# Spectral mixing and a bilinear GLU on one core: left-over rows stacked from group 3 on instead of 5, in five sets with their own scratch

## The chip, the core and the metric

The kernel runs as one launch on one core of a Trainium2 chip. The metric is device time in microseconds of that launch. The kernel before was timed three times: 671.66, 671.69 and 671.91 us, median 671.69 us. The profile is of another execution of the same program, which took 671.72 us; its span, from the first to the last instruction, is 669.9 us.

Engines are named as in the profile: PE is TensorE (matmuls), PEld its weight loads, DVE VectorE, ACT ScalarE, POOL GpSimd, SP SyncE. SP computes nothing; it issues transfers in program order, and a transfer that has to wait holds back all transfers written behind it.

## What is computed

Two blocks in sequence on x of shape (2048, 640) in float32. The first is layer normalisation, a real 2-D Fourier transform, a pointwise product with a complex filter, the inverse transform and the residual. The second is layer normalisation, a bilinear gated unit with 1728 hidden columns, and the residual.

```python
def _A_ref(x, w_r, w_i):
    X = jnp.fft.rfft2(x, axes=(-2, -1))
    X = X * (w_r + 1j * w_i)
    return jnp.fft.irfft2(X, s=(S, D), axes=(-2, -1))

def _B_ref(x, w_gate, w_up, w_down):
    h = jnp.einsum("bsd,df->bsf", x, w_gate) * jnp.einsum("bsd,df->bsf", x, w_up)
    return jnp.einsum("bsf,fd->bsd", h, w_down)

h  = x + _A_ref(_layernorm(x), A_w_r, A_w_i)
h2 = h + _B_ref(_layernorm(h), B_w_gate, B_w_up, B_w_down)
```

The change lies in the first block alone, in the transform along the 640 features.

## The kernel before

The sequence of 2048 rows is split as 16 times 128. A first stage transforms along 128 (the matmuls of line 270, to about 38 us of the span). Its result is cut into 16 **groups** of frequencies. The **feature stage** (about 38 to 100 us) then runs a loop over the groups g = 0 to 14, and each pass does for PE, in this order:

- `s2_mm(g)`, line 476: the transform along 16, from the tile `t` into the PSUM tile `u`. There is one `u` only, so this may write it no sooner than DVE has read the last one.
- `d_mm(g + 2)`, line 121 by the helper `mmx`: the transform along the 640 features. Folding has cut it into four "main" products of 128 rows (tile `s1`, tables `tab`), and a small rest of rows that don't fill 128. The rest is done in fp32r (a split into a high and a low part, three products).
- `is2_mm(g - 1)`, line 527: the inverse along 16, into `ir` (64 + 1 rows) and `im`.

DVE does `filt(g)` (lines 484 to 486: three products of `u` with the filter `wts`), the sum at line 493, and line 563. ACT copies `d_mm`'s result to `t` (line 465) and the inverse's result away (lines 545 and 556). So the loop is closed: `u` is written by PE, read by three DVE operations, and only then written again.

The rest of rows in `d_mm` exists in two forms:

- **Plain** (groups 0 to 4, `g < PLAIN`): six matmuls over 128 rows and 322 columns, read from `s1r`, which holds the high part in plane 0 and the low part in plane 1. The 128 rows are four quarters of 31 to 33 rows, and each quarter belongs to its own 160 to 194 columns of `re` or `im`; for the others the table holds zeros.
- **Stacked** (groups 5 to 15): the rows of one quarter are brought together three times over, as 33 high, 33 low and 33 high rows on 99 partitions. One matmul of 160 to 194 columns for each quarter then does the three products: four short matmuls instead of six long ones.

To stack rows on other partitions, they go through device memory. `spread(a, b)` writes the 33 rows of both planes for a range of groups to the scratch `sfar`, four transfers from SP, one for each quarter (line 445). `stack(g, n, tag)` reads n groups back, 66 partitions and 33 partitions in two transfers (line 455). The scratch is one tensor of shape [4 quarters, 2 planes, 33 rows, 11 groups, 128]; so one partition that is read gathers, for each quarter, a run of n x 512 bytes.

The order is written out by hand, and all these transfers are on SP's queue. Beside them SP issues for each pass two transfers of `bits` (the matrices of lines 476 and 527, line 417) and one or two of `wts` (the filter, lines 410 and 412). SP has eight semaphores for its transfers, used in turn: transfer k waits until transfer k - 8 has landed.

Before the loop, three pairs of ACT and DVE operations (lines 300 and 303) make the high and low parts of `s1r` for groups 0-1, 2-4 and 5-9, and a fourth pair, inside the loop, that of groups 10-15. `spread(5, 10)` is issued ahead of the loop, `stack` for groups 5-7 in pass 0, for groups 8-9 in pass 1, `spread(10, 16)` in pass 2, `stack` for 10-12 in pass 4 and for 13-15 in pass 7:

```python
PLAIN, MID = 5, 10
AGAIN = {0: (5, 3, "dC"), 1: (8, 2, "qt"), 4: (10, 3, 0), 7: (13, 3, 1)}
```

A tag names where the stacked rows stand in SBUF: `dC` and `qt` are free tiles, 0 and 1 are the two planes of `s1r` itself, whose groups 4 to 15 are overwritten once they have been spread.

Of the kernel before, what the change touches and what calls it, by code (L numbers as in the profile page):

```python
# [11 lines left out]
F32 = mybir.dt.float32  # L12
# [4 lines left out]
P = 128  # L17
S, D, NF, FF = 2048, 640, 321, 1728
NT = S // P
NG = 16  # L20
# [4 lines left out]
RROWS = ((31, 1), (0, 1), (62, 2), (63, 2))  # L25
RWHERE = ((1, 0), (0, 0), (1, 160), (0, 160))
RW = (160, 194, 162, 162)
PLAIN, MID = 5, 10
IPLAIN, IFAR = 5, 9
SUMS = 7  # L30
IPARTS = ((5, 4), (9, 3), (12, 4))
AGAIN = {0: (5, 3, "dC"), 1: (8, 2, "qt"), 4: (10, 3, 0), 7: (13, 3, 1)}
NR = 4
AHEAD = 5
FOLDS = {0: (1, 2), 1: (3,), 2: (4,), 7: (9,), 9: (11,)}
# [14 lines left out]
def f32(ap):  # L50
    return ap.bitcast(F32)
# [29 lines left out]
def tile_spectral_glu(ctx: ExitStack, tc: tile.TileContext, x, wre, wim, wgu, wlast, wdown, wdlast,  # L81
                      cc, ci, fmain, frem, imain, irem, mm, out):
    nc = tc.nc
# [4 lines left out]
    far = ctx.enter_context(tc.tile_pool(name="far", bufs=1, space=bass.MemoryType.DRAM))  # L88
# [60 lines left out]
    s1r = home("wA", [P, 2, NG, P], "s1r", F32R)  # L149
# [142 lines left out]
    def s1_rest(t):  # L292
        act(at(rest, t), PS1[t][1][:, 0:P].rearrange("p (g m) -> p g m", g=32), AF.Copy)
# [5 lines left out]
    def rest_high(a, b):  # L299
        act(s1r[:, 0, a:b], rest[:, a:b], AF.Copy)  # L300

    def rest_low(a, b):
        tt(s1r[:, 1, a:b], rest[:, a:b], f32(s1r[:, 0, a:b]), op=OP.subtract)
# [94 lines left out]
        s1_mm(t)  # L398
    s1_main(NT - 1, PS1[NT - 1][0], 2, 4)
    s1_rest(NT - 1)  # L400
    for a, b in ((0, 2), (2, PLAIN), (PLAIN, MID)):
        rest_high(a, b)
        rest_low(a, b)

# [2 lines left out]
    def load_w(g):  # L407
        w, j = wts[:, g % 3], g // 2 if g < NG - 2 else g - 7
        i = wts[:, 5 if j == 8 else 3 + j % 2]
        nc.sync.dma_start(w, wre[g])  # L410
        if g % 2 == 0 or g >= NG - 2:
            nc.sync.dma_start(i, wim[j])
        W2[g] = w, i

    def load_mm(g, way):
        if g < NG:
            nc.sync.dma_start(mms[g % 4][:, way], mm[g][:, way])
# [22 lines left out]
    ST = {}  # L440
    sfar = far.tile([4, 2, 33, NG - PLAIN, P], F32, name="sfar")

    def spread(a, b):
        for q, (r, s) in enumerate(RROWS):
            nc.sync.dma_start(sfar[q, :, :, a - PLAIN:b - PLAIN].rearrange("l r g n -> r l g n"),
                              f32(s1r[r:r + 32 * s + 1:s, :, a:b]))

    def stack(g, n, tag):
        if tag in (0, 1):
            o = s1r[:, tag, NG - 12:NG].rearrange("p (q n) m -> p q n m", q=4)  # L450
        else:
            o = home(tag, [P, 4, n, P], "st", F32R)
        src = sfar[:, :, :, g - PLAIN:g - PLAIN + n].rearrange("q l r g n -> q (l r) (g n)")
        for a, b, r in ((0, 66, 0), (66, 99, 0)):
            nc.sync.dma_start(f32(o[a:b].rearrange("p q g n -> p q (g n)")),
                              src[:, r:r + b - a].rearrange("q r n -> r q n"))
        for i in range(n):
            ST[g + i] = o[:, :, i]

    def d_out(g, parts=(0, 1)):  # L460
        for i in parts:
# [5 lines left out]
    def s2_mm(g):  # L467
        if g >= NG - 2:
            ps = PU[g] = bank("re"), bank("im")
        elif g == 0:  # L470
            ps = PU[g] = bank("im2", 1), bank("ir2", 1)
        else:
            PU[g] = pools["y"].tile([P, 2, 512], F32, tag="u", name="u", bufs=1)
            ps = PU[g][:, 0], PU[g][:, 1]
        for h in range(2):
            nc.tensor.matmul(ps[h][:, 0:NQ], mms[g % 4][:, 0, h], T[g][:, h], start=True, stop=True)  # L476
# [106 lines left out]
    for g in range(NG - 1):  # L583
        s2_mm(g)
        load_mm(g + 4, 0)
        if g + 2 < NG:
            d_mm(g + 2)
        if g + 3 == NG:
            xt = home("big", [P, 2, 5, 2, 512], "xt", F32R)
            flat = xt[:, 1].rearrange("p k l n -> p (k l n)")  # L590
            irt, sirt = cut(flat, 0, 5, NQ), cut(flat, 5 * NQ, 4, 162)
            scrap, near = cut(flat, 2258, D), cut(flat, 2258 + D, 4, 4, P)
        if g == NG - 2:
            nc.gpsimd.dma_start(flat[:, 0:2258], irem)
        if g == NG - 2:
            s2_mm(g + 1)
            filt_half(g, 0, True, (lambda: is2_out(g - 2),))
        if g >= 1:
            is2_mm(g - 1)
            load_mm(g + 3, 1)  # L600
        if g < NG - 2:
            add = filt(g)
        else:
            direct, _ = filt_half(g, 1)
            direct()
            late = [filt_half(g + 1, 0), filt_half(g + 1, 1, True)]
            high, end, low, main, edges = is2_parts(g - 1)
            late[0][0]()
            high(copy)
            end(copy)  # L610
            low()
            late[0][1]()
            late[1][1]()
            main(slice(0, 4))
            edges(nc.gpsimd)
        if g + 3 < NG:
            load_w(g + 3)
        if g >= 4 and g in AGAIN:
            stack(*AGAIN[g])
        if g == 0:  # L620
            rest_high(MID, NG)
        elif g == 1:
            rest_low(MID, NG)
            qr = home("qr", [P, 2, NT, P], "qr", F32R)
        if g + 2 < NG:
            d_out(g + 2, (0,))
            if 1 <= g < NG - 3:
                high, end, low, main, edges = is2_parts(g - 1)
                high(copy)
                end(copy)  # L630
            d_out(g + 2, (1,))
            add()
            if 1 <= g < NG - 3:
                low()
                main(slice(0, 4))
                edges(nc.gpsimd)
        if g < 2:
            stack(*AGAIN[g])
        elif g == 2:
            spread(MID, NG)  # L640
        if g == 9:
            nc.sync.dma_start(cit, ci)
            nc.sync.dma_start(imt, imain)
# [252 lines left out]
    for ts in (range(3), range(3, 6), range(6, 8)):  # L896
        n, t0 = len(ts), ts[-1] + 1
# [664 lines left out]
```

## Time and profile before

| what | value |
|---|---|
| median of three runs | 671.69 us |
| the profiled execution, whole | 671.72 us |
| its span | 669.9 us |
| granted TensorE clock | 0.999 of full speed |
| feature stage | about 38 to 100 us of the span |
| moved by DMA over the whole span | 66.12 MB in 48953 packets |

The profile has a page (busy time by engine, a chain of the work that ended last, groups of instructions) and views that are asked for: a timeline of one engine in order of time, busy time by window, and a table of waits. A row of a timeline reads: start in us, length in us, engine, line, operation, what it writes and from what, shape, count, and in brackets the idle time ahead of it with what ended it. SPq rows are the issuing of transfers, not the moving of bytes. Names such as `sfar<-s1r` are the program's tiles; `frt` and `tab` are tables.

### The profile page before, as it was taken

What the parts mean: (1) busy time and instruction counts of PE and PEld (TensorE: products, weight loads), DVE (VectorE), ACT (ScalarE), POOL (GpSimd) and SP (SyncE); (2) the same over time, 40 slices, a digit from 0 to 9 for tenths busy, and PEclk for the clock granted to TensorE, in tenths of its full rate; (3) what the DMA queues carried; (4) which work ended last, traced back from release to release, by engine and by line L of the source; (5) the groups of instructions that cost most, each with busy time, mean ns of one, the idle gap of its engine ahead of it and who ended that gap; (6) DMA issues with size and microseconds to landing.
All of it is one profiled execution on the core that took longest, in us unless ns stands there. A gap on an engine that the chain in (4) does not pass through costs nothing.

```text
span 669.9 us, 10244 instructions
## 1 busy us (share of the span) xinstructions
PE 661.1 (99%) x3695; PEld 588.4 (88%) x3695; DVE 469.1 (70%) x953; ACT 321.6 (48%) x621; POOL 394.1 (59%) x377
## 2 busy tenths in 40 slices
PE   7999999999999999999999999999999999999997
PEld 7999999887888888888888899888888888888887
DVE  6969997788767767594857567754757475757644
ACT  6977773585525244453626146534434251624220
POOL 3101124750397977968696445198786869697610
PEclk9999999999999999999999999999999999999999
DMA  8638874502212120142332467212011121212004
GB/s 316 230 111 279 245 250 144 172 2 79 79 40 80 39 79 21 33 105 60 98 79 83 95 132 261 79 40 73 14 37 75 41 78 40 79 40 80 1 0 158
DMA packets 48953, 66.12 MB, mean 99 GB/s; under 512 B 24082, under 2 KB 30670, under 8 KB 48774
## 3 DMA queue, kind: packets, MB, share of 16 engines
q1 hardware_dynamic: 48246, 62.91, 30.4%
q0 software_dynamic: 288, 2.16, 0.8%
q8 instruction: 29, 0.48, 0.3%
q10 hardware_dynamic: 368, 0.39, 0.2%
q14 instruction: 22, 0.18, 0.1%
HBM read 54.61 MB, written 10.84 MB: 98 GB/s over the span
## 4 chain that ended last, share of the span: by engine, by line
PE 95%; ACT 2%; DVE 2%; DMA 1%; issue 0%; DVEq 0%
PE e L121 50%; PE d L121 26%; PE eo L121 4%; PE y L121 2%; PE re L121 2%; PE u L476 2%; PE im L121 2%; PE im L527 2%; PE im L270 2%; PE ir L527 1%; DMA x<-in_x_dram 1%; ACT s L296 1%; ACT fold L212 0%; ACT fold L211 0%; PE y L803 0%
## 5 line engine op out<-in xcount | busy, mean ns | idle before, releaser
L121 PE MATMUL e<-xt,wst 128*128 128x512 f32 x864 | 211.1, 390 | 0.0
L121 PEld LDWEIGHTS e<-xt,wst 128*128 128x128 f32 x864 | 160.6, 188 | 31.7
L1082 DVE TENSOR_TENSOR x<-d,x 128x320 f32<-128x320 f32 x280 | 120.3, 482 | 41.2 <-PE d L121 37.0
L121 PE MATMUL d<-wd,ht 128*128 128x320 f32 x832 | 142.1, 309 | 0.0
L121 PEld LDWEIGHTS d<-wd,ht 128*128 128x128 f32 x832 | 129.6, 188 | 5.2
L996 POOL TENSOR_TENSOR wst<-raw,wst 128x1024 fp32r<-128x1024 f32 x23 | 55.5, 2412 | 69.4 <-ACT wst L995 69.4
L121 PE MATMUL e<-t,wst 128*128 128x512 f32 x360 | 94.0, 391 | 0.0
L121 PEld LDWEIGHTS e<-t,wst 128*128 128x128 f32 x360 | 66.7, 188 | 13.0
L121 PE MATMUL d<-wt,ht 128*128 128x320 f32 x360 | 68.9, 309 | 0.0
L1012 POOL TENSOR_TENSOR wst<-raw,wst 128x896 fp32r<-128x896 f32 (+1 forms) x46 | 65.3, 1445 | 0.2 <-ACT wst L1007 0.2
L121 PEld LDWEIGHTS d<-wt,ht 128*128 128x128 f32 x360 | 57.3, 188 | 0.8
L1098 ACT ACTIVATE ht<-e 128x512 fp32r<-128x512 f32 x44 | 26.4, 600 | 49.3 <-DVE e L1160 23.7
L1007 ACT ACTIVATE wst<-raw 128x896 fp32r<-128x896 f32 (+1 forms) x48 | 30.1, 676 | 31.2 <-POOL raw L1001 30.4
L1156 DVE TENSOR_TENSOR e<-e,h 128x512 f32<-128x512 f32 x24 | 16.8, 699 | 39.4 <-ACT wst L1007 23.2
L1057 DVE TENSOR_TENSOR x<-d,x 128x320 f32<-128x320 f32 x62 | 27.5, 485 | 22.5 <-PE d L121 22.4
L688 ACT ACTIVATE wd<-draw 128x320 fp32r<-128x320 f32 (+1 forms) x30 | 15.7, 561 | 55.2 <-POOL draw L698 52.4
L121 PE MATMUL e<-xt,wdir 128*128 128x512 f32 x180 | 41.9, 392 | 0.0
L1136 ACT ACTIVATE h<-e 128x512 f32<-128x512 f32 x24 | 14.3, 596 | 56.8 <-PE e L121 56.8
L121 PEld LDWEIGHTS e<-xt,wdir 128*128 128x128 f32 x180 | 33.4, 188 | 7.5 <-ACT xt L813 0.5
L1101 DVE TENSOR_TENSOR ht<-e,ht 128x512 fp32r<-128x512 f32 x54 | 36.9, 685 | 1.6 <-ACT ht L1098 1.3
L1153 ACT ACTIVATE h<-e 128x512 f32<-128x512 f32 x24 | 14.3, 597 | 46.6 <-PE e L121 46.6
L667 POOL TENSOR_TENSOR wd<-draw,wd 128x640 fp32r<-128x640 f32 x8 | 12.5, 1582 | 40.8 <-ACT wd L666 40.8
(241 smaller groups left out, 1190.6 us busy)
## 6 DMA issues: line engine op xcount, KB each, us to landing
raw<-in_wgu_dram SPq DMA_DIRECT2D x24, 640.0 KB
draw<-in_wdown_dram SPq DMA_DIRECT2D x24, 320.0 KB
wts<-in_wre_dram SPq DMA_DIRECT2D x16, 322.0 KB
x<-in_x_dram SPq DMA_DIRECT2D x15, 320.5 KB
out_dram<-x SPq DMA_DIRECT2D x15, 320.0 KB
bits<-in_mm_dram SPq DMA_DIRECT2D x32, 128.0 KB
wts<-in_wim_dram SPq DMA_DIRECT2D x9, 322.0 KB
zfar<-zr SPq DMA_DIRECT2D x32, 80.0 KB
```

The costliest lines, as they stand in the source:

```text
L121: nc.tensor.matmul(o, l, r, start=start, stop=stop, skip_group_check=True)
L527: nc.tensor.matmul(out, y[:, h, a:b], inv(g, h), start=n == 0, stop=n == len(ys) - 1)
L688: act(o[:, 0, a:a + n], src, AF.Copy)
L996: ptt(wa[:, 1], stage[:, 0:1024], f32(wa[:, 0]), op=OP.subtract)
L1007: act(ws[:, 0, o:o + b - a], stage[:, a:b], AF.Copy)
L1012: ptt(ws[:, 1, o:o + b - a], stage[:, a:b], f32(ws[:, 0, o:o + b - a]), op=OP.subtract)
L1057: tt(xv, ps[b][:, 0:320], xv, op=OP.add)
L1082: tt(xv, o, xv, op=OP.add)
L1098: act(hop[:, a, 0], src, AF.Copy)
L1101: engine.tensor_tensor(hop[:, a, 1], src, f32(hop[:, a, 0]), op=OP.subtract)
L1136: act(h0, oa, AF.Copy)
L1156: tt(ob, ob, h1, op=OP.add)
```

## The change

Stacking starts at group 3 instead of group 5. The eleven, now thirteen, stacked groups are cut into five sets (3-5, 6-7, 8-10, 11-13, 14-15), and each set has a scratch tensor of its own, in the order [plane, row, quarter, group, 128]. A partition that is read then finds its four quarters in one run of n x 2048 bytes, where before there were four runs of n x 512. The transfers of `spread` write runs of n x 512 bytes, n being 3 or 2, where before they wrote 5 x 512 and 6 x 512.

```diff
-PLAIN, MID = 5, 10
+PLAIN, NEXT, MID = 3, 6, 10
-AGAIN = {0: (5, 3, "dC"), 1: (8, 2, "qt"), 4: (10, 3, 0), 7: (13, 3, 1)}
+SETS = ((3, 3, "dC"), (6, 2, "qt"), (8, 3, 0), (11, 3, 1), (14, 2, "dC"))
+SPREAD, AGAIN = {1: (2,), 2: (3, 4)}, {1: 1, 3: 2, 6: 3, 8: 4}
...
-    for a, b in ((0, 2), (2, PLAIN), (PLAIN, MID)):
+    for a, b in ((0, 2), (PLAIN, NEXT), (2, PLAIN), (NEXT, MID)):
         rest_high(a, b)
         rest_low(a, b)
...
-    sfar = far.tile([4, 2, 33, NG - PLAIN, P], F32, name="sfar")
+    sfar = [far.tile([2, 33, 4, n, P], F32, name="sfar") for _, n, _ in SETS]
 
-    def spread(a, b):
+    def spread(i):
+        g, n, _ = SETS[i]
         for q, (r, s) in enumerate(RROWS):
-            nc.sync.dma_start(sfar[q, :, :, a - PLAIN:b - PLAIN].rearrange("l r g n -> r l g n"),
-                              f32(s1r[r:r + 32 * s + 1:s, :, a:b]))
+            nc.sync.dma_start(sfar[i][:, :, q].rearrange("l r g n -> r l g n"),
+                              f32(s1r[r:r + 32 * s + 1:s, :, g:g + n]))
...
-        src = sfar[:, :, :, g - PLAIN:g - PLAIN + n].rearrange("q l r g n -> q (l r) (g n)")
+        src = sfar[i].rearrange("l r q g n -> (l r) (q g n)")
         for a, b, r in ((0, 66, 0), (66, 99, 0)):
-            nc.sync.dma_start(f32(o[a:b].rearrange("p q g n -> p q (g n)")),
-                              src[:, r:r + b - a].rearrange("q r n -> r q n"))
+            nc.sync.dma_start(f32(o[a:b].rearrange("p q g n -> p (q g n)")), src[r:r + b - a])
...
-    spread(PLAIN, MID)
+    spread(0)
+    stack(0)
+    spread(1)
...
-        if g >= 4 and g in AGAIN:
-            stack(*AGAIN[g])
+        if g >= 3 and g in AGAIN:
+            stack(AGAIN[g])
...
-        if g < 2:
-            stack(*AGAIN[g])
-        elif g == 2:
-            spread(MID, NG)
+        if g == 1:
+            stack(AGAIN[g])
+        for i in SPREAD.get(g, ()):
+            spread(i)
```

Three places of the instruction order matter. The first is PE in pass 1, `d_mm(3)`, from its last main product to the first product of `is2_mm(0)`. Before:

```order
L121 MATMUL re_634<-tab_87,s1_89 128x161
L121 MATMUL re_634<-frt_88,s1r_90 128x322
L121 MATMUL im_635<-frt_88,s1r_90 128x322
L121 MATMUL re_634<-frt_88,s1r_90 128x322
L121 MATMUL im_635<-frt_88,s1r_90 128x322
L121 MATMUL re_634<-frt_88,s1r_90 128x322
L121 MATMUL im_635<-frt_88,s1r_90 128x322
L527 MATMUL ir2_647<-bits_94,y_611 65x32x4 x2
```

And the same place now (`st` is the tile of the stacked rows):

```order
L122 MATMUL re_644<-tab_87,s1_89 128x161
L122 MATMUL im_645<-frt_88,st_566 128x160
L122 MATMUL re_644<-frt_88,st_566 128x194
L122 MATMUL im_645<-frt_88,st_566 128x162
L122 MATMUL re_644<-frt_88,st_566 128x162
L529 MATMUL ir2_655<-bits_94,y_624 65x32x4 x2
```

Six long matmuls have become four short ones, which read `st` where the six read `s1r`. The same holds for `d_mm(4)`, one pass later.

The second place is SP's queue from the end of the load of the first matrices to the second read of stacked rows. Before:

```order
L445 DMA sfar_542<-s1r_90 33x2x640 x4
L417 DMA bits_94<-in_mm_dram 128x256
L410 DMA wts_93<-in_wre_dram 128x644
L455 DMA st_627<-sfar_542 66x4x384
L455 DMA st_627<-sfar_542 33x4x384
L417 DMA bits_94<-in_mm_dram 128x256 x2
L410 DMA wts_93<-in_wre_dram 128x644
L412 DMA wts_93<-in_wim_dram 128x644
L455 DMA st_676<-sfar_542 66x4x256
L455 DMA st_676<-sfar_542 33x4x256
```

Now:

```order
L447 DMA sfar_544<-s1r_90 33x2x384 x4
L458 DMA st_566<-sfar_544 66x1536
L458 DMA st_566<-sfar_544 33x1536
L447 DMA sfar_545<-s1r_90 33x2x256 x4
L418 DMA bits_94<-in_mm_dram 128x256
L411 DMA wts_93<-in_wre_dram 128x644
L418 DMA bits_94<-in_mm_dram 128x256 x2
L411 DMA wts_93<-in_wre_dram 128x644
L413 DMA wts_93<-in_wim_dram 128x644
L458 DMA st_684<-sfar_545 66x1024
L458 DMA st_684<-sfar_545 33x1024
```

The first read of stacked rows has moved ahead of a transfer of `bits` and one of `wts`, to right behind the writes that it waits for; four writes of a second set have come in between.

The third place is SP's queue behind that, up to the read of the set of groups 8 to 10. Now:

```order
L447 DMA sfar_546<-s1r_90 33x2x384 x4
L418 DMA bits_94<-in_mm_dram 128x256 x2
L411 DMA wts_93<-in_wre_dram 128x644
L447 DMA sfar_547<-s1r_90 33x2x384 x4
L447 DMA sfar_548<-s1r_90 33x2x256 x4
L418 DMA bits_94<-in_mm_dram 128x256 x2
L411 DMA wts_93<-in_wre_dram 128x644
L413 DMA wts_93<-in_wim_dram 128x644
L458 DMA s1r_90<-sfar_546 66x1536
L458 DMA s1r_90<-sfar_546 33x1536
```

Before, one set of four writes stood here (of 768 columns), and no read: groups 8 and 9 had been read already, and the next read was that of groups 10 to 12, a pass later. On ACT and DVE one operation of lines 300 and 303 has become two (640 columns are now 128 and 512), and groups 3-5 come second in their order.

More of the change, by code (lines that the diff above doesn't have):

```diff
@@ L440, in tile_spectral_glu, with stack @@
     ST = {}
-    sfar = far.tile([4, 2, 33, NG - PLAIN, P], F32, name="sfar")
-    def spread(a, b):
+    sfar = [far.tile([2, 33, 4, n, P], F32, name="sfar") for _, n, _ in SETS]
+    def spread(i):
+        g, n, _ = SETS[i]
         for q, (r, s) in enumerate(RROWS):
-            nc.sync.dma_start(sfar[q, :, :, a - PLAIN:b - PLAIN].rearrange("l r g n -> r l g n"),
-                              f32(s1r[r:r + 32 * s + 1:s, :, a:b]))
-    def stack(g, n, tag):
+            nc.sync.dma_start(sfar[i][:, :, q].rearrange("l r g n -> r l g n"),
+                              f32(s1r[r:r + 32 * s + 1:s, :, g:g + n]))
+    def stack(i):
+        g, n, tag = SETS[i]
         if tag in (0, 1):
@@ L452, in stack @@
             o = home(tag, [P, 4, n, P], "st", F32R)
-        src = sfar[:, :, :, g - PLAIN:g - PLAIN + n].rearrange("q l r g n -> q (l r) (g n)")
+        src = sfar[i].rearrange("l r q g n -> (l r) (q g n)")
         for a, b, r in ((0, 66, 0), (66, 99, 0)):
-            nc.sync.dma_start(f32(o[a:b].rearrange("p q g n -> p q (g n)")),
-                              src[:, r:r + b - a].rearrange("q r n -> r q n"))
-        for i in range(n):
-            ST[g + i] = o[:, :, i]
+            nc.sync.dma_start(f32(o[a:b].rearrange("p q g n -> p (q g n)")), src[r:r + b - a])
+        for j in range(n):
+            ST[g + j] = o[:, :, j]
     def d_out(g, parts=(0, 1)):
```

## The prediction

> **What bounds the kernel now.** I read the page first: busy time by engine, then the chain of the work that ended last. Then I went to the feature stage alone, by windows and by the timeline of one engine.
>
> ```profile
> PE 661.1 (99%) x3695; PEld 588.4 (88%) x3695; DVE 469.1 (70%) x953; ACT 321.6 (48%) x621; POOL 394.1 (59%) x377
> PE 95%; ACT 2%; DVE 2%; DMA 1%; issue 0%; DVEq 0%
> 48.74:53.20 4.46, 4.46 (x33) 1.00 0.85 250
> 57.17:61.16 3.99, 3.99 (x31) 1.00 0.83 284
> ```
>
> PE is busy 99% of the span and is 95% of the chain, so a microsecond taken from PE is a microsecond of the kernel, unless something else is late next. The last two rows are PE alone (length, busy, granted clock, DMA share, GB/s): a pass with a plain `d_mm` takes 4.46 us, one with a stacked `d_mm` 3.99 us, at full clock. Two plain passes become stacked. But DMA engines are 85% busy there, and DVE has work of its own. Here is PE from `d_mm(3)` (plain) to the fourth `u`:
>
> ```profile
> 47.74 0.42 PE L121 MATMUL re<-frt,s1r 128*128 128x322 f32 x1
> 48.74 0.60 PE L527 MATMUL ir<-bits,y 128*65 128x128 f32 x4
> 50.07 1.25 PE L476 MATMUL u<-t,bits 128*128 128x322 f32 x4
> 54.52 1.25 PE L476 MATMUL u<-t,bits 128*128 128x322 f32 x4
> 56.65 0.35 PE L121 MATMUL im<-frt,st 99*128 99x160 f32 x1
> 57.17 0.60 PE L527 MATMUL ir<-bits,y 128*65 128x128 f32 x4
> 58.51 1.26 PE L476 MATMUL u<-t,bits 128*128 128x322 f32 x4
> ```
>
> Start to start, the plain rest takes 48.74 - 47.74 = 1.00 us, the stacked one 57.17 - 56.65 = 0.52 us. And DVE beside it:
>
> ```profile
> 49.46 0.96 DVE L303 TENSOR_TENSOR s1r<-rest,s1r 128x768 fp32r<-128x768 f32 x1
> 53.36 0.82 DVE L486 TENSOR_TENSOR us<-u,wts 64x644 f32<-64x644 f32 x1
> 55.81 0.83 DVE L484 TENSOR_TENSOR y<-u,wts 128x644 f32<-128x644 f32 x1 [0.32 <-PE u L476]
> 57.51 0.82 DVE L486 TENSOR_TENSOR us<-u,wts 64x644 f32<-64x644 f32 x1
> ```
>
> From u at 54.52 to `filt` at 55.81 are 1.29 us, `filt` ends at 58.33, and the next u starts 0.18 us later, at 58.51. So the loop u, `filt`, u closes in 3.99 us, just what PE's own work takes. Neither has slack to make up what is lost.
>
> **What the shorter `d_mm` saves.** Two times 1.00 - 0.52 us are 0.96 us of PE work. Both fall between u(1) and u(3), and u(3) may not start before DVE has finished `filt(2)`, at 53.36 + 0.82 = 54.18. DVE comes to that through `filt(1)`, the extra operation at 49.46 and the sum, none of which the change shortens, and it idles only afterwards (0.32 us). With the 0.18 us from DVE's end to u, u(3) can start at 54.36 at the soonest, where it started at 54.52. **At most 0.16 us are saved**; the other 0.80 us turn into a wait for DVE. After u(3) every pass is of the same kind as before, 3.99 us.
>
> **Whether group 3 is there in time.** Its first stacked matmul would start at 47.74. If the rows come at S, u(2) starts at S + 0.52 + 1.33 (from 48.74 to 50.07), and u(3) 3.99 us later, at S + 5.84. It breaks even with 54.52 at S = 48.68: 0.94 us of lateness cost nothing, and each microsecond beyond costs one. S is worked out from these rows, the queue and its waits:
>
> ```profile
> 39.39 0.97 DVE L303 TENSOR_TENSOR s1r<-rest,s1r 128x256 fp32r<-128x256 f32 x2 [2.62 <-ACT s1r L300]
> 41.29 2.54 SPq L445 DMA_DIRECT2D sfar<-s1r  x4
> 46.69 0.76 SPq L455 DMA_DIRECT2D st<-sfar  x2
> SPq L455 <- DMA sfar<-s1r: 0.9, 1, 0.9
> 107.04 2.19 SPq L716 DMA_DIRECT2D ifar<-qr  x4
> 111.28 0.29 SPq L727 DMA_DIRECT2D xt<-ifar  x1
> SPq L727 <- DMA ifar<-qr: 1.2, 1, 1.2
> 194.24 0.33 SPq L984 DMA_DIRECT2D raw<-in_wgu_dram  x1
> 198.21 1.06 ACT L995 ACTIVATE wst<-raw 128x1024 fp32r<-128x1024 f32 x1 [0.63 <-DMA raw<-in_wgu_dram]
> ```
>
> - Start. The second DVE operation will be that of groups 3-5, with the same 384 columns; it ends at 39.39 + 0.97 = 40.36. The four writes start at 40.39 instead of 41.29.
> - Write. Before, four writes of 5 groups took from 41.29 until the read behind them went out at 46.69, which waited for nothing else (0.9 us for the writes): 5.40 us. Now they carry three fifths of the bytes. Were only bytes to count, that is 3.2 us; were only their number, 5.4. The nearest row is between: the same kind of writes with runs of 2048 bytes went from 107.04 to 111.28, 4.24 us for five of them, some of it another wait. I take 3.9: the read goes out at 44.3.
> - Read. No read of 99 partitions in runs of 6144 bytes is in the trace. The nearest is the weight load of 640 KB in runs of 5120 bytes on an idle queue, issued at 194.24 and used by ACT, which waited for it, at 198.21: 3.97 us. Ours is 594 KB in two transfers, the second 0.38 us later: 4.35 us, with a lower end of 4.0. The upper end is the round trip of the set of groups 8 and 9, in a full queue, below: 5.4. So the rows are there at 48.65, and with 0.18 us for PE's release S = 48.83: **0.15 us lost** (u(3) at 54.67). The ends are S = 47.8 (on time) and 51.4 (2.7 us lost).
>
> [...] The trace has the same amount read in runs of 1536 bytes on an otherwise quiet queue, issued at 121.08 (`si`; the weight load stands first, and the column before the last is the share of 16 DMA engines):
>
> ```profile
> 195.00:196.00 1.00, 1.00 (x7) 0.91 (x6) 0.55 (x2) 0.47 (x1) 0.92 (x2) 1.00 0.72 164
> 196.00:197.00 1.00, 1.00 (x6) 0.80 (x5) 1.00 (x3) 0.02 (x1) 0.89 (x2) 1.00 0.92 374
> 197.00:198.00 1.00, 1.00 (x6) 0.84 (x5) 0.13 (x1) 0.58 (x1) 0.95 (x2) 1.00 0.30 118
> 121.08 0.32 SPq L727 DMA_DIRECT2D si<-ifar  x1
> 122.00:123.00 1.00, 1.00 (x9) 0.92 (x8) 0.96 (x5) 0.63 (x2) 0.97 (x1) 1.00 0.56 99
> 123.00:124.00 1.00, 1.00 (x7) 0.76 (x6) 1.00 (x2) 0.30 (x1) 0.98 (x1) 1.00 0.71 241
> 124.00:125.00 1.00, 1.00 (x10) 1.00 (x9) 1.00 (x4) 0.87 (x2) 1.00 (x2) 1.00 0.75 191
> 125.00:126.00 1.00, 1.00 (x7) 0.84 (x7) 0.97 (x3) 0.97 (x4) 0.79 (x2) 1.00 0.29 80
> ```
>
> It kept the engines 2.31 us busy, against 1.94 us for the 640 KB in long runs, and moved until after 125.0, 3.9 us behind its issue, against 3.3. [...]
>
> **Whether the later sets are in time.** The set of 6-7 is read from the same place in the queue as 8-9 before; the four writes put ahead of it fit into a wait of SP for PE:
>
> ```profile
> 47.49 3.13 SPq L417 DMA_DIRECT2D bits<-in_mm_dram  x2
> 52.48 0.83 SPq L455 DMA_DIRECT2D st<-sfar  x2
> 57.88 0.80 SPq L445 DMA_DIRECT2D sfar<-s1r  x1
> SPq L445 <- DMA st<-sfar: 0.6, 1, 0.6
> 60.64 0.35 PE L121 MATMUL im<-frt,st 99*128 99x160 f32 x1
> 68.61 0.35 PE L121 MATMUL im<-frt,st 99*128 99x160 f32 x1
> ```
>
> SP's transfer at 57.88 waited for the landing of the read issued at 52.48: a round trip of 5.4 us. Such a read lands near 58; group 6 needs it at 60.64. The set of 8-10 is the tight one. Group 8 needs it at 68.61. From 52.48 on, 21 transfers stand ahead of its read, where 13 stood: 9 of the usual kind at 0.42 us each (0.83 for two) and 12 writes, at between 0.42 and 0.64 us (2.54 for four; now they are smaller). At 0.53 us that gives 52.48 + 3.8 + 6.4 = 62.7. The read also waits for the last writes: four transfers earlier, at 61.0, the last was issued, and 46.69 - 41.29 - 2.54 = 2.86 us later it has landed, at 63.9. With 4.35 and 0.18 us the rows are there at 68.4, just in time; at 0.64 us they would be 1.3 us late, at 0.42 us 1.3 us early. As only lateness counts, I take **0.3 us lost**; the ends are 0 and, with a read of 5.4 us, 2.4. Sets 11-13 and 14-15 are issued some 9 us and more ahead of use; I cost them at nothing, and `wts` and `bits`, asked for two passes and more ahead, too. One operation more on ACT and on DVE ahead of the loop costs at most 0.3 us each; ACT's is covered, since PE's second half of u(0) starts later than `t` is done:
>
> ```profile
> 41.42 0.89 ACT L465 ACTIVATE t<-im 64x322 f32<-64x322 f32 x2
> 43.04 0.71 PE L476 MATMUL ir<-t,bits 128*128 128x322 f32 x2
> ```
>
> DVE idles 2 us there. Without the cover it would be 0.1 to 0.3 us.
>
> **The sum**, against the execution's own 671.72 us (the median of the runs is 671.69, so they agree): 671.72 + 0.15 + 0.3 = **672.2 us**. What a measurement of this kernel can tell from no change is about 0.2%, 1.34 us.
>
> **Rivals.** All is on time: the 0.16 us of DVE's limit, 671.6 us. For it speaks the short run of bytes of set 3-5; against it that S must be under 48.5. The full 0.96 us, 670.8 us, would need DVE to reach `filt(2)` sooner, and no row shows how. **The transfers are late**, the rival on the slower side: PE stands before `d_mm(3)` and again before `d_mm(8)`, because eight more issues ahead of the read make SP the bound of that set and DMA engines are 85% busy. It decides from S = 48.68 and from rows for group 8 later than 68.6 us. [...] For it speaks the busy share; against it that long runs were cheaper. [...]
>
> **Chances.** Small loss, up to 1.3 us: 0.46. All on time: 0.19. Full saving: 0.04. Late transfers: 0.27. Something faster that I don't see: 0.04. Faster by over 0.2% is the last case alone, 0.04; slower by over 0.2% the late transfers, 0.27; within it the rest, 0.69. The range, 671.4 to 674.3, leaves out the full saving, the unseen gain and about a third of the late case, 0.17 together.
>
> **What would show it.** PE's timeline after: the step from line 121 on `st` to line 527 in `d_mm(3)` and `d_mm(4)` at 0.52 us; an interval without matmuls ahead of the first, as long as S - 47.74; u(3) at 54.4 to 54.7. SP: the first read at about 44.3, that of set 8-10 near 64. Wrong would be: u(3) before 54.3, or a wait of PE at a group other than 3 and 8.

## The result

The changed kernel takes 681.81 us (median of four runs, 680.79 to 683.48), the kernel before 671.8 us on the same chip: a ratio of 1.0149, 95% interval 1.0137 to 1.0162. It is 10 us slower. The profiled execution has a span of 679.0 us, 9.1 us above that of before, and the explanation below is made for these 9.1 us. It is the fastest of the four; of the other three, with a granted clock down to 0.992, there is no trace.

First the page of the changed kernel, busy time and the chain of work that ended last:

```profile
span 679.0 us, 10259 instructions
PE 662.2 (98%) x3691; PEld 588.5 (87%) x3691; DVE 468.6 (69%) x954; ACT 321.6 (47%) x622; POOL 394.2 (58%) x377
PE 91%; DMA 3%; ACT 2%; DVE 2%; SPq 1%; issue 0%; DVEq 0%
```

PE's share of the chain has fallen from 95% to 91%, and DMA and SP's issuing stand in its place. Where, is seen in PE's timeline: the two rows with a wait (in brackets, with what ended it), and the `u` products around them.

```profile
45.65 1.25 PE L478 MATMUL u<-t,bits 128*128 128x322 f32 x4
50.16 0.31 PE L122 MATMUL im<-frt,st 99*128 99x160 f32 x1 [2.11 <-DMA st<-sfar]
55.96 1.26 PE L478 MATMUL u<-t,bits 128*128 128x322 f32 x4
67.92 1.26 PE L478 MATMUL u<-t,bits 128*128 128x322 f32 x4
75.52 0.47 PE L122 MATMUL im<-frt,s1r 99*128 99x160 f32 x1 [5.20 <-DMA s1r<-sfar]
76.44 1.05 PE L529 MATMUL ir<-bits,y 128*65 128x128 f32 x4
78.99 1.79 PE L478 MATMUL u<-t,bits 128*128 128x322 f32 x4
83.52 1.26 PE L478 MATMUL u<-t,bits 128*128 128x322 f32 x4
```

Both waits are for stacked rows, at the two groups that the prediction named, 3 and 8. u(3) starts at 55.96 us instead of 54.52: **1.44 us lost** by the first set. The rest of group 8 would have started at 70.06 us (every stacked pass repeats after 3.99 us) and starts at 75.52: **5.46 us**. And then it is slow: the first product of `ir` has 1.05 us instead of 0.60. From the rest of group 8 to that of group 9 there are 80.62 - 75.52 = 5.10 us up to the next main products, where the same stretch in other passes takes 2.95: **2.15 us**. Together 9.05 us. PE's windows say why it is slow (length, busy, granted clock, DMA share, GB/s):

```profile
72.50:73.00 0.50, 0.00 (x0) 1.00 1.05 243
73.00:73.50 0.50, 0.00 (x0) 0.76 1.08 259
73.50:74.00 0.50, 0.00 (x0) 0.50 1.09 233
79.50:80.00 0.50, 0.50 (x2) 0.50 0.00 0
80.00:80.50 0.50, 0.50 (x3) 0.92 0.47 82
```

The granted clock fell to half while PE waited, and stayed there until about 80.1 us, long after the rows had come: by the two windows in which it changed, half clock lasted from 73.26 to 80.08 us, 6.82 us. No term of the prediction held this.

SP's queue in the same stretch, where one row is a run of transfers and the second column the time that issuing them took:

```profile
53.74 0.72 SPq L458 DMA_DIRECT2D st<-sfar  x2
54.56 2.67 SPq L447 DMA_DIRECT2D sfar<-s1r  x4
57.33 0.95 SPq L418 DMA_DIRECT2D bits<-in_mm_dram  x2
58.88 0.33 SPq L411 DMA_DIRECT2D wts<-in_wre_dram  x1
59.44 5.47 SPq L447 DMA_DIRECT2D sfar<-s1r  x8
65.03 1.00 SPq L418 DMA_DIRECT2D bits<-in_mm_dram  x2
66.12 0.38 SPq L411 DMA_DIRECT2D wts<-in_wre_dram  x1
66.59 0.38 SPq L413 DMA_DIRECT2D wts<-in_wim_dram  x1
67.14 0.71 SPq L458 DMA_DIRECT2D s1r<-sfar  x2
```

SP issues almost without a pause for 14 us. The read of groups 8 to 10 goes out at 67.14 us, and PE gets its rows at 75.52, 8.4 us later. Twelve writes cost SP 2.67 + 5.47 = 8.14 us, 0.68 each. While it issues the last of them, the engines that move bytes are mostly idle:

```profile
64.00:65.00 1.00, 1.00 (x5) 1.00 0.32 95
65.00:66.00 1.00, 1.00 (x8) 1.00 0.24 68
```

During the read itself they are not: the share of DMA time was 1.05 to 1.09 in the windows from 72.5 to 74 us above (it sums the times of packets and can pass 1), and 0.99 on the mean of 67.14 to 75.52 us. Between them:

```profile
70.00:72.00 2.00, 0.33 (x3) 1.00 0.88 219
```

So the runs were to test theory Q: the read of groups 8 to 10 goes out too late, because of SP's issues and their order, and is then as slow as any read in this traffic. Its rivals are B, that the bytes themselves run short, and L, that the layout does it. Theory C: the slow pass is PE's clock after a wait.

### The profile page after: what moved, and what is told of

Read it like the earlier page. It is cut to its first block, busy times and chain, and to the rows that moved or that the text cites. A ratio compares the mean times of both kernels' runs of the same rounds, so it can differ in the third digit from the quotient of the medians.

```text
span 679.0 us, 10259 instructions
## 1 busy us (share of the span) xinstructions
PE 662.2 (98%) x3691; PEld 588.5 (87%) x3691; DVE 468.6 (69%) x954; ACT 321.6 (47%) x622; POOL 394.2 (58%) x377
## 4 chain that ended last, share of the span: by engine, by line
PE 91%; DMA 3%; ACT 2%; DVE 2%; SPq 1%; issue 0%; DVEq 0%
PE e L122 50%; PE d L122 26%; PE eo L122 4%; PE y L122 2%; PE u L478 2%; PE im L529 2%; PE im L271 2%; PE re L122 1%; PE im L122 1%; DMA s1r<-sfar 1%; PE ir L529 1%; DMA st<-sfar 1%; DMA x<-in_x_dram 1%; ACT s L297 1%; ACT fold L213 0%
```

## The experiments

Times are medians; the kernel before stood at 671.7 to 671.95 us beside all of them. The edits are against the changed kernel unless said otherwise.

**The layout alone taken back.** Five sets as in the changed kernel, but each read gathers four runs again.

```diff
-    sfar = [far.tile([2, 33, 4, n, P], F32, name="sfar") for _, n, _ in SETS]
+    sfar = [far.tile([4, 2, 33, n, P], F32, name="sfar") for _, n, _ in SETS]
...
```

> The changed kernel with its five sets and its order of issue, but each set's scratch in the old order (quarter, plane, row, group), so that a read gathers four runs of n x 512 bytes again. Theory Q (the rows of groups 8 to 10 are late because their read stands behind too many issues on SP, and is then as slow as any read in the full queue): the same writes and the same queue, so the same time within 1 us of 681.8, the read of groups 8 to 10 issued near 67 and PE's wait for it near 5 us. Rival L (the contiguous layout itself makes the reads slow): the reads are 2 us or more shorter, PE's two waits shrink, 678 us or less. Rival L' (contiguous runs help, as I assumed in the prediction): the reads are some tenths longer, 682 to 683 us.

682.16 us, ratio 1.0150 (1.0131 to 1.0168): the same as the changed kernel. Read out at 68.13, rows used at 75.98 us:

```profile
50.30 0.31 PE L122 MATMUL im<-frt,st 99*128 99x160 f32 x1 [2.28 <-DMA st<-sfar]
68.13 0.75 SPq L458 DMA_DIRECT2D s1r<-sfar  x2
75.98 0.47 PE L122 MATMUL im<-frt,s1r 99*128 99x160 f32 x1 [3.85 <-DMA s1r<-sfar]
```

7.85 us with four short runs, 8.38 with one long run; for the first set 5.5 and 5.35 (from 44.79 and 44.81). PE's wait for group 8 is 3.85 us and not near 5 because half clock after the first wait, from 51.13 to 54.55 us, had put PE 1.8 us behind the changed kernel. Both L are out: the layout neither costs nor helps here.

**The layout alone given to the kernel before** (sets from group 5 on, its order of issue).

```diff
-    sfar = far.tile([4, 2, 33, NG - PLAIN, P], F32, name="sfar")
+    sfar = {g: far.tile([2, 33, 4, n, P], F32, name="sfar") for g, n in SETS.items()}
...
-    spread(PLAIN, MID)
+    spread(5)
+    spread(8)
...
-            spread(MID, NG)
+            spread(10)
+            spread(13)
```

> The kernel before with its stacking from group 5 on and its order of issue, but with a contiguous scratch for each of its four sets, so 16 writes instead of 8 and reads of one run. Theory Q: the eight writes more cost SP some 5 us (0.68 us each), but each read still has slack here (read of 5 to 7 out near 49.4 and landed by 55, needed at 56.6; read of 10 to 12 out near 66 and landed by 73.7, needed near 76.6), so 671.7 us within 0.2%. Rival L (the layout is what costs): PE waits at group 5 or 10 and the time is 2 us or more above.

674.0 us, ratio 1.0033 (1.002 to 1.0046), single runs from 672.03 to 676.82: slower, where no change was expected. The profiled execution is the slowest of the ten. In it PE waited for no rows, but its `u` of one pass was late, since DVE stood before it for the filter:

```profile
69.77 0.83 DVE L485 TENSOR_TENSOR y<-u,wts 128x644 f32<-128x644 f32 x1 [2.17 <-PE ir L528]
71.75 0.83 DVE L486 SCALAR_TENSOR_TENSOR us<-u,wts 64x644 f32<-64x644 f32 x1 [1.16 <-DMA wts<-in_wim_dram]
73.52 2.23 PE L477 MATMUL u<-t,bits 128*128 128x322 f32 x4 [2.92 <-issue]
```

The wait of 2.17 us is put down to PE, which had long been done; by the trace's semaphore events the load of `wts` for this pass landed at 69.67. It had been issued at 66.37, behind eight writes that kept SP from 57.06 to 64.83 us. So what stands behind writes, here `wts`, can come late when every set of rows is in time. But 2.8 us of this SP stood waiting for earlier transfers to land, and the two reads ahead had been slow in this run (last section); how much is due to the number of writes and how much to these reads is not shown.

**The eight writes for groups 11 to 15 behind the read of 8 to 10**, which goes to the free tile `dC`, since it may no longer overwrite their rows.

```diff
-SETS = ((3, 3, "dC"), (6, 2, "qt"), (8, 3, 0), (11, 3, 1), (14, 2, "dC"))
-SPREAD, AGAIN = {1: (2,), 2: (3, 4)}, {1: 1, 3: 2, 6: 3, 8: 4}
+SETS = ((3, 3, "dC"), (6, 2, "qt"), (8, 3, "dC"), (11, 3, 0), (14, 2, "qt"))
+SPREAD, AGAIN = {1: (2,), 3: (3, 4)}, {1: 1, 3: 2, 6: 3, 8: 4}
```

> The changed kernel, with the eight writes for groups 11 to 15 issued behind the read of groups 8 to 10 instead of ahead of it (that read goes to another free tile, so that it doesn't overwrite what is still to be spread). Theory Q: SP no longer spends 5.5 us on them there; the read can't go out before PE's is2_mm(2) ends, near 64, and two bits and two wts after it, so it goes out near 65.3 instead of 67.1, and takes 7 to 8 us behind the wts: PE's second wait is 2.5 to 3.5 us instead of 5.3. If PE's clock then stays at full speed, as it did after the first wait of 2.1 us, the time is 675.5 to 677 us, with a clock that falls 677 to 679 us. Rival (the read is slow for itself, wherever it stands): issued 1.8 us sooner but landing no sooner than 1 us before now, 680 us or more.

677.11 us, ratio 1.0083 (1.0062 to 1.0105). The time is that expected, the way is not. The read went out at 62.03 us, sooner than I had expected, and PE's wait for group 8 is gone: by the semaphore events the rows landed at 69.16, and they are asked for at 69.60 us. Instead DVE waited one pass later:

```profile
76.15 0.83 DVE L486 TENSOR_TENSOR y<-u,wts 128x644 f32<-128x644 f32 x1 [3.55 <-DMA wts<-in_wre_dram]
78.78 1.56 PE L478 MATMUL u<-t,bits 128*128 128x322 f32 x4 [3.17 <-issue]
```

The eight writes keep SP from 62.82 to 70.13 us, 1.9 us of it a wait for the read ahead to land; the load of `wts` behind them goes out at 71.23 and is needed at 72.6. Moved writes only choose who waits.

**PE kept at work in the second wait.**

```diff
-        parts(ps, main, [])
+        for _ in range(4 if g == 8 else 1):
+            parts(ps, main, [])
```

> The changed kernel, with the four main products of d_mm(8) done four times instead of once (8 matmul pairs more of 1.33 us for each four; each repetition starts its accumulation anew), so that PE works through some 4 us of its second wait. Theory C (a lasting idle of PE lowers its clock, and the pass from 75.5 to 80.6 took 5.10 us instead of 2.95 for that reason): the wait left is 1 to 2 us, the granted clock stays at 1.0 there, the pass takes 2.95 us again, and the time falls by some 2.1 us to about 679.7. Rival (the slow pass comes from the transfers that arrive then, not from idling): the pass stays near 5 us and the time at 681.8 us.

678.96 us, ratio 1.0108 (1.0091 to 1.0125), 2.85 us less than the changed kernel. The clock stays at 1.0 behind the second wait, of which 1.29 us is left. But in this execution it had fallen behind the first wait, of 1.83 us:

```profile
51.00:51.50 0.50, 0.50 (x7) 0.89 0.90 302
54.50:55.00 0.50, 0.50 (x4) 0.70 0.76 283
75.00:76.50 1.50, 0.21 (x2) 1.00 1.00 268
```

Half clock from 51.39 to 54.80 us, 3.41 us, although PE had been working again since 49.81. C holds: where PE works through most of the wait, the stretch behind it is as fast as any (76.39 to 79.30 us, 2.91).

**The writes of the last four sets on POOL.**

```diff
-            nc.sync.dma_start(sfar[i][:, :, q].rearrange("l r g n -> r l g n"),
+            (nc.gpsimd if i else nc.sync).dma_start(sfar[i][:, :, q].rearrange("l r g n -> r l g n"),
```

> The changed kernel, with the sixteen writes of its last four sets issued by POOL, which has little to do in this stage, instead of SP. Sets, layout, reads and bytes are the same. Theory Q (SP's time is what runs short: a write costs it 0.68 us whatever its size, and what stands behind, a read, bits or wts, comes late): the read of groups 8 to 10 goes out by 62 us and its rows are there before PE asks for them; the second wait is gone, and with it the half clock behind it; the first wait of 1.8 to 2.3 us stays, since set 3-5 is written and read as before. Time 672.7 to 675 us, the upper end if the first wait lowers the clock. Rival B (the moving of the bytes is what runs short): the same packets through the same engines, a second wait of 3 us or more, 677 us or more.

680.66 us, ratio 1.013 (1.0116 to 1.0143): hardly better, and a miss for Q as I had put it. SP was free, yet the read stood:

```profile
59.99 4.93 POOL L447 DMA_DIRECT2D sfar<-s1r  x8
63.38 0.40 SPq L413 DMA_DIRECT2D wts<-in_wim_dram  x1
68.24 0.71 SPq L458 DMA_DIRECT2D s1r<-sfar  x2
```

From 63.4 to 68.24 us it waited for the writes of groups 11 to 15, for it overwrites their rows (its tile is a plane of `s1r`). In the changed kernel this condition was met at 66.4 us by the semaphore events, 0.7 us before SP came to the read: two conditions end almost together, and taking one away shows the other. The second wait is 2.00 us, the read having taken 6.4 us (68.24 to 74.65); the first grew to 2.94 us, where 1.8 to 2.3 were expected, and half clock followed both (52.31 to 55.72 us, and 3.4 us of the stretch from 70 to 80 us). A write takes POOL 0.62 us, hardly less than the 0.68 of SP.

**Fewer writes.** One scratch in the old order, spread for 3-5, 6-9 and 10-15: 12 writes in place of 20.

```diff
-    sfar = [far.tile([2, 33, 4, n, P], F32, name="sfar") for _, n, _ in SETS]
+    sfar = far.tile([4, 2, 33, NG - PLAIN, P], F32, name="sfar")
...
-    spread(0)
-    stack(0)
-    spread(1)
+    spread(PLAIN, NEXT)
+    stack(0)
+    spread(NEXT, MID)
...
-        for i in SPREAD.get(g, ()):
-            spread(i)
+        if g == 2:
+            spread(MID, NG)
```

> Stacking from group 3 in the same five sets, reads at the same places, but one scratch in the order of the kernel before, so that one batch of four writes serves groups 6 to 9 and another groups 10 to 15: 12 writes instead of 20, with the same bytes. Theory Q: four writes instead of twelve stand ahead of the read of groups 8 to 10 after 52 us, it goes out by 62.5 us, and the second wait is gone; the first stays at 1.8 to 2.3 us; 672.7 to 675 us. Rival B (bytes, not the number of issues): the second wait stays at 3 us or more, 677 us or more.

677.35 us, ratio 1.0079 (1.0062 to 1.0096). The read goes out at 65.17 us, not 62.5, and the second wait is 1.98 us, not 5.2; half clock followed both waits (51.08 to 54.49 us, and 3.4 us of the stretch from 70 to 80 us):

```profile
65.17 0.76 SPq L457 DMA_DIRECT2D s1r<-sfar  x2
74.28 0.31 PE L122 MATMUL im<-frt,s1r 99*128 99x160 f32 x1 [1.98 <-DMA s1r<-sfar]
```

Neither theory's number: with fewer writes the read goes out 1.97 us sooner, but its rows are used only 1.24 us sooner, 9.1 us behind the issue. The first wait and its half clock had already put PE 2.0 us behind the changed kernel's times, which shortens the second wait, and SP's loads of `bits` wait for PE (10.0 us in all between 50 and 80 us).

**From group 4, 8 writes, one scratch** (against the kernel before), and the same with POOL for one operation:

```diff
-PLAIN, MID = 5, 10
+PLAIN, MID = 4, 10
-AGAIN = {0: (5, 3, "dC"), 1: (8, 2, "qt"), 4: (10, 3, 0), 7: (13, 3, 1)}
+AGAIN = {0: (4, 3, "dC"), 1: (7, 2, "qt"), 4: (9, 3, 0), 7: (12, 3, 1), 9: (15, 1, "qt")}
```

> The kernel before with stacking from group 4 instead of 5, in sets 4-6, 7-8, 9-11, 12-14 and 15 from its one scratch: 8 writes as before, one read more late in the stage. Group 4 needs its rows at 52.2 us, and they come near 52.2 or before. One plain rest less, 0.48 us of PE work. By the prediction's limit of DVE (u(3) may not start before filt(2) has ended) at most 0.16 us come through: u(3) at 54.36 to 54.52, time 671.5 to 671.75 us. Rival (no such limit): u(3) at 54.04, 671.2 us. Rival (late rows): a wait of PE ahead of d_mm(4) or d_mm(9), above 672 us.

673.7 us, ratio 1.0028 (1.0018 to 1.0038). Writes of six groups ahead of the read: it goes out at 47.72 us, and PE waits 1.59 us for group 4, until 54.09: the rival of late rows. DVE's limit can't be seen behind that.

```diff
-            rest_low(MID, NG)
+            nc.gpsimd.tensor_tensor(s1r[:, 1, MID:NG], rest[:, MID:NG], f32(s1r[:, 0, MID:NG]), op=OP.subtract)
```

> As the one from group 4, with the low part of groups 10 to 15 made by POOL instead of DVE. DVE then comes to filt(2) 0.8 us sooner. By the theory of DVE's limit the rest of the 0.48 us now comes through: u(3) near 54.0 to 54.1 and the time 0.3 us or so below the one from group 4, 671.2 us. Rival: PE's own order or the rows bound it, and nothing changes against that one.

673.67 us, ratio 1.0025 (1.0016 to 1.0035): the rows of group 4 again, at 53.70. These two are bound by the rows and say nothing of DVE.

**Both conditions away: writes on POOL, and 8-10 to the free tile `dC`.**

```diff
-SETS = ((3, 3, "dC"), (6, 2, "qt"), (8, 3, 0), (11, 3, 1), (14, 2, "dC"))
+SETS = ((3, 3, "dC"), (6, 2, "qt"), (8, 3, "dC"), (11, 3, 0), (14, 2, "qt"))
...
+            (nc.gpsimd if i else nc.sync).dma_start(sfar[i][:, :, q].rearrange("l r g n -> r l g n"),
```

> The run with its writes on POOL, and in it the set 8-10 goes to a free tile, so that its read no longer waits until groups 11 to 15 have been spread (there it stood from 63.4 to 68.24 us for that). Nothing of SP's time or of a tile's release now holds the read: it goes out near 64 us. Theory Q (issue and order alone make group 8 late): its rows land by 71 us, no wait ahead of d_mm(8) above 0.5 us and none of DVE for wts; only the first wait of 2 to 3 us and the half clock behind it are left, 673.5 to 675.5 us. Rival B (with two groups more of scratch the engines that move bytes are short in 55 to 76 us, and a read in that traffic takes 8 us or more wherever it stands): a wait of 1 us or more stays, of PE for the rows or of DVE for wts, 676 us or more.

676.71 us, ratio 1.0071 (1.0058 to 1.0084). The second wait is gone but for some 0.3 us, and none of DVE for `wts` is there; the time is higher than Q gave because the first wait grew to 2.9 us and was followed by half clock for 6.83 us (50.60 to 57.43): u(3) at 59.88, 5.36 us late. The writes of 6-7 on POOL now run beside those of 3-5: by the semaphore events the last of these landed at 45.11 instead of 44.66 us, and the read behind took 5.5 instead of 5.2.

```profile
50.93 0.47 PE L122 MATMUL im<-frt,st 99*128 99x160 f32 x1 [2.91 <-DMA st<-sfar]
50.50:51.00 0.50, 0.07 (x1) 0.60 0.92 331
65.53 0.71 SPq L458 DMA_DIRECT2D st<-sfar  x2
```

This run doesn't decide between Q and B. The read of groups 8 to 10 landed at 74.20, 8.7 us behind its issue, as B gave, and the time is B's too; its rows are in time because PE itself came so late.

**Half of the filter's bytes.** The kernel leaves out half of the columns of the filter for groups 3 to 10; its result is not the reference's.

```diff
-        nc.sync.dma_start(w, wre[g])
+        h = slice(0, 1 if 3 <= g <= 10 else 2)
+        nc.sync.dma_start(w[:, h], wre[g][:, h])
```

(and the same for `wim`)

> The changed kernel with half of the filter left out: the loads of wts for groups 3 to 10 bring the first half of their columns alone, so the filtered result is not the reference's; number and order of issues are the same, some 160 KB less for each such load. Rival B (bytes): the traffic of 55 to 76 us falls by a quarter to a third, the read of groups 8 to 10 takes 5 to 6 us instead of 8.2, and the second wait shrinks to 2 us or less. Theory Q: the read still goes out at 66 to 67.5 us, since SP's issues are the same, and though it is faster, the second wait stays at 3 us or more.

678.45 us, ratio 1.0099 (1.0079 to 1.012). Single runs go from 676.58 to 681.06, and the profiled execution is the slowest of them; what made the others faster is in no trace. DMA moved 183 GB/s in 60 to 70 us instead of 214, some 14% less, where a quarter to a third was expected, and the issue times are nearly the same:

```profile
67.50 0.71 SPq L459 DMA_DIRECT2D s1r<-sfar  x2
75.04 0.47 PE L122 MATMUL im<-frt,s1r 99*128 99x160 f32 x1 [3.18 <-DMA s1r<-sfar]
```

The rows came at 75.04 instead of 75.52 us, though the read went out 0.36 us later: it took 7.54 instead of 8.38 us. The wait is 2 us shorter, but mostly because half clock after the first wait, from 50.63 to 54.05 us, had put PE 1.5 us later. So the bytes count in the length of the read, by 0.84 us for this much of them, and the read is still too late by its issue. B didn't come as put (5 to 6 us), but with half of the cut that was meant it isn't refuted.

**From group 4 with the first set spread and read by itself** (against the run from group 4), without and with POOL for the low part:

```diff
-    for a, b in ((0, 2), (2, PLAIN), (PLAIN, MID)):
+    for a, b in ((0, 2), (PLAIN, 7), (2, PLAIN), (7, MID)):
...
-    spread(PLAIN, MID)
+    spread(PLAIN, 7)
+    stack(*AGAIN[0])
+    spread(7, MID)
...
```

> Stacking from group 4, with the one scratch, but groups 4 to 6 are spread and read first, as set 3-5 is in the changed kernel, and groups 7 to 9 then (12 writes). The rows of group 4 come at 49.7 to 50.5 us, as those of set 3-5 did, and are asked for at 52.2: no wait there. Then the prediction's limit of DVE can be seen: u(3) at 54.36 us, not before (54.52 in the kernel before), and 671.5 to 671.8 us if no later set is late. Rival (no such limit): u(3) at 54.04 us, 671.2 us. Rival (the four writes more delay what follows): a wait of PE at a later group, 672.5 us or more.

> The same, with the low part of groups 10 to 15 made by POOL instead of DVE, which then reaches filt(2) some 0.9 us sooner. If DVE is what holds u(3), it now starts at 54.0 to 54.1 us, and the time is 0.3 us below the run before it, 671.2 us or so. If not, nothing changes against that run.

672.11 us, ratio 1.0008 (0.9999 to 1.0018), and 672.93 us, ratio 1.0013 (1.0004 to 1.0023). Now group 4 is in time, and DVE's limit stands open: PE's third `u`, and DVE's last product before it, first with the low part on DVE, then on POOL:

```profile
53.28 0.82 DVE L486 TENSOR_TENSOR us<-u,wts 64x644 f32<-64x644 f32 x1
54.20 1.32 PE L476 MATMUL u<-t,bits 128*128 128x322 f32 x4
```

```profile
52.96 0.82 DVE L486 TENSOR_TENSOR us<-u,wts 64x644 f32<-64x644 f32 x1
53.95 1.26 PE L476 MATMUL u<-t,bits 128*128 128x322 f32 x4
```

With DVE doing it, u(3) comes 4.21 us after u(2) (at 49.99); with POOL 3.99 (u(2) at 49.96), which is PE's own pass. The gain at u(3) is kept in neither median: in the first the read of 9-11, behind four more writes, came 1.52 us late at 74.15; the second, expected 0.3 us below the first, is 0.8 us above it in the median; it has no such wait in its profile (672.07 us), but single runs from 671.30 to 675.68, and what happens in the longer ones is not shown. None of the kernels beats the one before.

**The first wait filled too** (against the run with POOL and the free tile): the main products of d_mm(3) three times.

```diff
-        parts(ps, main, [])
+        for _ in range(3 if g == 3 else 1):
+            parts(ps, main, [])
```

> The run with its writes on POOL and the free tile for the set 8-10, whose only wait was the 2.9 us ahead of d_mm(3), with the four main products of d_mm(3) done three times, so that PE works through 2.7 us of that wait. There the rows came at 50.93 us; by S + 5.84 us that alone puts u(3) 2.25 us later than before, and the half clock from 50.7 to 57.1 us made it 5.36. Theory C (half of the loss that is left is the clock after the wait): the clock stays at 1.0, u(3) starts near 56.8 us, and the time is 674 to 674.5 us. Rival (the passes were slow for another reason, bits, wts or the transfers): 676.5 us, as without the filling.

674.92 us, ratio 1.005 (1.0036 to 1.0063), a little above the 674 to 674.5 of theory C; the profiled execution 673.95, its span 672.2 us. The clock stays full (1.00 from 45 to 80 us), and what is left is the lateness of the rows alone:

```profile
51.05 0.31 PE L122 MATMUL im<-frt,st 99*128 99x160 f32 x1 [0.68 <-DMA st<-sfar]
52.86 1.25 PE L479 MATMUL u<-t,bits 128*128 128x322 f32 x4
56.84 1.26 PE L479 MATMUL u<-t,bits 128*128 128x322 f32 x4
```

u(3) at 56.84 is 2.32 us late, and the span is 2.3 us longer: after that no pass loses anything. Without the filling u(3) was 3.04 us later, and the read of 8-10 went out at 65.53 instead of 62.50 us, 3.03 later: SP's queue waits for PE, so what PE loses is handed on to the transfers behind.

The runs by what they lost up to u(3) and from there to u(8), in us, from the starts of `u` (before: u(3) at 54.52, five passes later u(8) at 74.45):

| run | to u(3) | u(3) to u(8) | span, against 669.9 |
|---|---|---|---|
| the changed kernel | 1.44 | 7.63 | +9.1 |
| writes on POOL | 3.77 | 3.91 | +7.7 |
| fewer writes | 3.42 | 3.85 | +7.1 |
| writes on POOL, free tile | 5.36 | 0.32 | +5.5 |
| the same, first wait filled | 2.32 | 0 | +2.3 |

What they show of group 8 together: by the semaphore events the read of its set took 8.2 us from issue to landing in the changed kernel, 7.1 with the eight writes behind it, and 6.3, 9.0, 8.7 and 8.2 in the four lower rows of the table. The like read of groups 10 to 12 took 7.4 us in the kernel before already. So the change made it little slower; what it took away is the lead. Before, that read went out at 63.53 us for a use at 76.59, 13 us later; now it goes out at 67.14 for a use due at 70.06, 2.9 us later. So far Q is shown: sent at 62.03 us, with the eight writes behind it, the read was in time. Why such a read takes 6 to 9 us in this stage, where the one of set 3-5 takes 5.2, no run isolates.

## Why the prediction was wrong

- **What bounds, and PE's saving: right.** The rest takes 0.52 us now, and it brings nothing.
- **The limit of DVE: the mechanism right, its size a little off.** At most 0.16 us were to come through; the run from group 4 with its rows in time got 4.45 - 4.21 = 0.24 us, and the remaining 0.22 us only when an operation was taken off DVE. From DVE's end to u(3) are 0.10 us there, at 54.10 and 54.20; the 0.18 of the sum came from a pass that PE's own 3.99 us bound as well. In the changed kernel it never mattered, since the rows were later.
- **Set 3-5: the mechanism right, both terms too small.** The write took 40.42 to 44.81 us, 4.39 instead of 3.9; the read 5.2 instead of 4.35, from 44.81 to PE's release. S is 50.16 instead of 48.83, the loss 1.44 us instead of 0.15; inside the ends given (47.8 to 51.4). The `si` read that the prediction shows had the right price: by the semaphore events its second transfer landed at 126.28, 5.2 us behind the issue at 121.08, not 3.9.
- **Set 8-10: here the prediction failed.** The rows were to be there at 68.4 us and were used at 75.52, 7.1 us later. The read went out 3.2 us later than the 63.9 of the sum: the start at 52.48 was taken from the kernel before, but the read ahead of it now went out at 53.74; the twelve writes took 0.68 us each instead of 0.53, above my upper end of 0.64; and the usual transfers took more than 0.42 (0.95 and 1.00 us for two of `bits`). And the read was priced at 4.35 us plus the release, from a weight load on an idle queue; it took 8.38, 3.85 more. The right row was in the trace of before: the read of groups 10 to 12, issued at 63.53 us in the same traffic, landed at 70.97 by the semaphore events, 7.4 us. The upper end, 5.4, was that of a set of two groups, and of the first of its two transfers only: the second landed at 58.84, 6.4 us behind the issue. So the term of 0.3 us, with ends of 0 and 2.4, came out as 5.46.
- **A condition not named.** The read overwrites rows that the last eight writes still have to spread. The sum had the wait for the writes, but not that no shift in the queue gets round it.
- **The clock: no term for it.** A wait was priced at its length. Behind the second wait the half clock cost 2.15 us more, and the runs that filled a wait with matmuls show that it is the wait that brings it: the clock was 1.00 behind both waits so filled, and the pass took 2.91 us instead of 5.10 behind the one, u(3) came 3.04 us sooner behind the other.
- **The layout: wrong.** I had long runs some tenths cheaper. The run with four runs of 1536 bytes is as fast, 682.16 us against 681.81, and its read of groups 8 to 10 took 7.85 us against 8.38. The two windows that I had compared had different traffic beside them: an older weight load landed until 122.53, beside the short runs, while the long ones ran alone.
- **The rivals.** "The transfers are late" was the right case, with its places and its cause, and it got a chance of 0.27. The range ended at 674.3 us, 2.6 us above the kernel before, where 9.1 us came in the profiled execution. It was built on prices from quieter places than the one in question.

## What to carry to other kernels

A transfer is priced by the row of the same kind in the same traffic, up to the landing of its last part (here 7.4 us, not 4.35), and a queue by what issuing costs there: here twelve small writes cost SP 8.14 us, 0.68 each, and what stood behind them paid, a read (out at 67.14 us, not 63.9) or a load of the filter (DVE stood 3.55 us for it with the writes moved). Before stacking sooner or in more sets, ask what lead each read has, and which loads lose theirs. In this kernel, where PE is over 90% of the chain, a wait cost up to about twice its length, through the clock (2.91 us of wait put u(3) 5.36 us late); so a change that saves half a microsecond of matmuls and makes a wait possible has a poor bargain.

## What the runs showed of the hardware

- In a row of four or eight, a write of 66 runs cost its issuer 0.59 to 0.69 us on the mean where nothing else held it, with little regard to the length of the runs (single ones on SP 0.29 to 0.95): four took 2.54 us of SP before, with 2560 bytes each, 2.54 in the changed kernel with 1536, four with 1024 took 2.36, and eight with 1536 and 1024 took 5.47; on POOL four took 2.49 us.
- In the feature stage half clock came in pieces of 3.4 or 6.8 us, read from the granted clock in windows, and not by the length of a wait alone. After PE's first wait it lasted from 51.39 to 54.80 us where the wait was 1.83 us (the second one filled), 50.63 to 54.05 with 1.97 us (half of the filter's bytes), 51.13 to 54.55 with 2.28 us (the layout taken back), 51.08 to 54.49 with 2.49 us (fewer writes), 52.31 to 55.72 with 2.94 us (writes on POOL) and 50.60 to 57.43 with 2.91 us (the free tile as well). The clock stayed full after 2.11 us in the changed kernel, 1.79 us with the eight writes behind the read, 1.59 us in the run from group 4, and 1.52 us at group 9 with its first set read by itself. Half clock began up to 1.6 us after PE was at work again (49.81 and 51.39 us in the first of these runs), and lasted on while PE was busy. In the run with the layout taken back a second piece lasted from about 75.0 to 81.9 us. Why 1.83 us brought half clock and 2.11 us did not is not shown.
- In the run that gave the kernel before the new layout, the two reads of long runs took 7.5 to 9.7 us by the semaphore events, and 4.5 to 5.9 in four short runs before. Beside the changed kernel the two layouts were alike. What makes the difference stays open.
